# An S4D convolution and a token mixer on one core: the second chunk's selecting table made on chip, weight blocks and x's rows loaded at other places, the first piece's sums on VectorE

## The chip, the cores and the metric

The kernel runs on one core of a Trainium2 chip. The core has TensorE (PE, the matrix engine, whose weight loads are listed apart as PEld), VectorE (DVE), ScalarE (ACT), GpSimd (POOL) and SyncE (SP, which issues most transfers), an on-chip memory of 128 partitions (SBUF), matrix accumulators (PSUM), and 16 DMA engines between them and the memory outside (HBM). The metric is the device time of one execution in microseconds (us), the median over runs. A profiled execution gives the trace; its own time is a little above the median.

## The reference

One block with two halves, on 2048 tokens of 448 channels. The first half is a layer norm with modulation and a long convolution whose kernel comes from 256 complex exponentials per channel, done as an FFT of length 4096. The second is a layer norm and a token-mixing MLP.

```
P = exp((A * dt)[:, :, None] * pos)
K = 2 * einsum("dn,dnl->dl", C, P).real
y = irfft(rfft(u, 2L) * rfft(K, 2L), 2L)[:L]
x = x + ga * (y + u * D_skip)
h = layernorm(x) * (1 + cb) + sb
U = gelu(einsum("sd,sf->df", layernorm(h), w1) + b1)
x = x + gb * (einsum("df,fs->ds", U, w2) + b2)
```

## The kernel before

The FFT of length 4096 is split into 32 frequencies `k1` of 64 points each. The channels go in two chunks of 224. For each chunk there are 16 *pieces*, each of two `k1` values; the second chunk's have the numbers 16 to 31 (`NP` is 16). The first chunk's pieces run beside the generation of the convolution kernel; the second chunk's, which the change is about, run alone in a loop behind it.

A piece passes through these steps. `pc_load(n)` (L749) loads `u`, the input's spectrum, 224 KB, into one of five buffers. `pc_s2(n)` (L780) is eight small matmuls that finish the kernel's spectrum `kx`. `pc_mul(n, e0, e1)` multiplies: VectorE makes the products `zx` and `zy` (L789), and then two engines given as arguments make the difference (L791) and the sum (L792) of the complex product. In before both are GpSimd, for all pieces but the last (31), where both are VectorE. `zx` and `zy` have two buffers each. `pc_tables(n)` (L769, L770) makes the inverse's second table on ScalarE. `pc_inv(n)` (L806) is the inverse transform's eight matmuls, `pc_out(n)` copies the result from PSUM into `vt` on ScalarE (L812) and writes it to the HBM buffer `v_d` (L816), 224 KB. `vt` has four buffers in the second chunk, so the copy of piece n waits for the write of piece n - 4.

The loop takes `m` from 16 to 32 in steps of two (a *round*): matmuls and products of pieces `m` and `m + 1`, then inverse and write of `m - 2` and `m - 1`. PE, ACT, DVE and POOL follow the program's order throughout. SyncE's order is the program's too within this part. All of SP's transfers go through one queue.

Into the loop other loads are woven, in before at these rounds: at 18 the table `fl` (512 KB, L1276); at 20 and 22 `ln_first` (L1179), the first chunk's half of token rows 0 and 1; at 22 and at 24 one block of the MLP's first weights each (`wst.load`, L191; 448 KB in two transfers of 64 partitions); at 28 `x_pair(0)` (L1162), x's rows 0 and 1 (448 KB, also in two transfers).

`fl` is the selecting table. The last transform turns `v_d` into token rows; for rows 0 and 1, the last two pieces' share is taken from their `vt` tiles on chip, not from HBM (`ln_direct`, L1214 and L1216), so that the rows needn't wait for the last writes. `fl` picks out of a `vt` tile's 128 partitions what belongs to row r. It has 128 x 1024 numbers, nearly all zero; others are copies of one small table.

Behind the loop: `ln_second` (L1182) loads the rest of rows 0 and 1, which needs the pieces up to 29 written; `ln_main` (L1222) ends their transform; `ln_load(2)`, `(3)` (L1173) load rows 2 and 3, which need all pieces; then `x_pair(2)`, further weights, the layer norms (`y_sum` L1199, `ln_mod`, `ln_out`) and the MLP (`mlp1`, L1326 to L1328). The norms of rows from 2 on run beside the MLP's first half. A weight block is split by ScalarE (L211) and VectorE (L220) into a high and a low part before use.

Of the kernel before, what the change touches and what calls it, by code (L numbers as in the profile page):

```python
# [22 lines left out]
P = 128  # L23
# [9 lines left out]
NP = 16  # L33
# [6 lines left out]
def dft_tables():  # L40
    n1 = np.arange(32)
    k1 = np.arange(32)
    n2 = np.arange(64)
    k2 = np.arange(64)
    nn = 4096
    t = {}
    w = 2 * np.pi * np.outer(n1, k1) / 64
    w1 = np.zeros((2, 32, 32))
    w1[0] = np.cos(w)
    w1[1] = -np.sin(w)  # L50
    w1[0, :, 0] = 1
    w1[1, :, 0] = (-1.0) ** n1
    wc = np.zeros((4, 32, 2, 4, 32))
    for g in range(4):
        for c in range(2):
            wc[g, :, c, g, :] = w1[c]
    wu = np.zeros((2, 2, 32, 32, 2, 2))
    for a in range(2):
        wu[:, a, ..., a] = w1.transpose(1, 2, 0)
    t["WU"] = wu.reshape(P, P)  # L60

    t["WC"] = wc.reshape(P, 2, 2, 2, 32).swapaxes(3, 4).reshape(P, 2 * P)
    s = np.zeros((2, 64, 32, 2, 64))
    i1 = np.zeros((2, 64, 32, 2, 64))
    i2 = np.zeros((2, 64, 32, 2, 64))

    def inverse(rows, cols, k, m, ang):
        a = np.cos(ang) * 2 / nn
        b = np.sin(ang) * 2 / nn
        i1[0, rows, k, m[0]] = a  # L70
        i1[1, rows, k, m[0]] = -b
        i2[1, rows, k, m[0]] = -a
        i2[0, rows, k, m[0]] = -b
        if len(m) > 1:
            i1[0, rows, k, m[1]] = b
            i1[1, rows, k, m[1]] = a
            i2[1, rows, k, m[1]] = -b
            i2[0, rows, k, m[1]] = a

    for k in range(1, 32):  # L80
        ang = 2 * np.pi * np.outer(n2, k + 64 * k2) / nn
        s[0, :, k, 0] = np.cos(ang)
        s[1, :, k, 0] = np.sin(ang)
        s[0, :, k, 1] = -np.sin(ang)
        s[1, :, k, 1] = np.cos(ang)
        inverse(slice(None), None, k, (0, 1), ang.T)


    for q in range(32):
        ang = 2 * np.pi * n2 * (32 + 64 * q) / nn  # L90
        s[1, :, 0, 0, q] = np.cos(ang)
        s[1, :, 0, 1, q] = -np.sin(ang)
        inverse(q, None, 0, (1,), ang)
    for q in range(33, 64):
        ang = 2 * np.pi * n2 * (64 * (q - 32)) / nn
        s[0, :, 0, 0, q] = np.cos(ang)
        s[0, :, 0, 1, q] = -np.sin(ang)
        inverse(q, None, 0, (0,), ang)
    s[0, :, 0, 0, 32] = 1
    s[0, :, 0, 1, 32] = (-1.0) ** n2  # L100
    i1[0, 32, 0, 0] = 1 / nn
    i2[1, 32, 0, 0] = (-1.0) ** n2 / nn
    s2 = s.reshape(P, 32 * P)

    su = s.swapaxes(3, 4).reshape(2, 64, 32, P)
    t["S2"] = su.reshape(2, 2, 2, 16, 32 * P).swapaxes(1, 2).reshape(P, 32 * P)

    one = np.einsum("cnk,cqkm->km", w1, su)
    t["SV"] = one[ones_k1()].T

    order = lambda a: a.reshape(P, 32, 2, 2, 2, 16).swapaxes(3, 4).reshape(2, 64, 32, P)
    v1, v2 = order(i1), order(i2)
    pairs = v1.reshape(2, 64, NP, 2, P).transpose(3, 1, 2, 0, 4).reshape(P, NP, 2 * P)
    t["SI"] = np.concatenate([s2.reshape(P, NP, 2 * P), pairs], 2).reshape(P, NP * 4 * P)
    t0 = np.zeros((P, 2, P))
    t0[32, 0] = v1[0, 32, 0] + v2[1, 32, 0]
    t0[:, 1] = pairs[:, 0, P:]
    t["T0"] = t0.reshape(P, 2 * P)
    ft = np.zeros((32, 2, 2, 32, 2))
    w = 2 * np.pi * np.outer(k1, n1) / 64  # L120
    f0 = np.cos(w)
    f1 = -np.sin(w)
    f0[0] = 1
    f1[0] = (-1.0) ** n1
    for h in range(2):
        ft[:, 0, h, :, h] = f0
        ft[:, 1, h, :, h] = f1
    t["FT"] = ft.reshape(P, 64)

    fl = np.zeros((2, 2, 2, 16, 2, 4, 2, 32, 2))  # L130
    for r in range(2):
        for g in range(2):
            fl[:, :, g, r, r, :, g] = ft[28:].transpose(1, 2, 0, 3, 4)
    t["FL"] = fl.reshape(P, 8 * P)


    te = np.zeros((3, 64, 16, 32))
    tg = np.zeros((3, 16, 4, 16, 32))
    n = np.arange(32)
    for d in range(16):  # L140
        te[0, 2 * d : 2 * d + 2, d] = 2 * n + 1
        te[2, 2 * d : 2 * d + 2, d] = -n
        tg[0, d, 0:2, d] = n
        tg[0, d, 2:4, d] = 1
        tg[2, d, 0:2, d] = -64 * n
        tg[2, d, 2:4, d] = 1
    tg = tg.reshape(3, 16, 2, 2, 512).swapaxes(1, 2)
    tt = np.concatenate([te.reshape(3, 64, 512), tg.reshape(3, 64, 512)], 1)
    tt[1] = -tt[0]
    t["TT"] = tt.reshape(3, P, 512)  # L150
    return {k: np.ascontiguousarray(v.astype(np.float32)) for k, v in t.items()}


def ones_k1():

    return [0] + list(range(1, 32, 2))
# [7 lines left out]
def token_pair(a, r, g):  # L164

    rows = a.rearrange("(n g h r) d -> g n h (r d)", g=2, h=2, r=16)
    return rows[g, :, :, r * D : (r + 2) * D]
# [58 lines left out]
def tile_adaln_s4d_mixer(ctx, tc, i, out):  # L226
    nc = tc.nc
# [13 lines left out]
    ft = cp.tile([P, 64], F32, name="ft")  # L241
# [5 lines left out]
    with ExitStack() as es:  # L247
        V, S, G, T = nc.vector, nc.scalar, nc.gpsimd, nc.tensor
# [85 lines left out]
        for q in range(4):  # L334
            r = slice(32 * q, 32 * q + 1)
# [422 lines left out]
        def pc_keep(p):  # L758

            nc.sync.dma_start(kept(p)[:, 0 : 3 * P], si[:, p, 0 : 3 * P])  # L760

        def pc_tables(n):

            real, h = pt[n][0], P // 2
            if n == NP:
                pt[n] = real, t0[:, 1]
                return
            imag = fp.tile([P, P], F32, tag="bt", name="bt", bufs=3)
            S.activation(imag[:, 0:h], real[:, h:P], AF.Copy, scale=-1.0)  # L769
            S.copy(imag[:, h:P], real[:, 0:h])  # L770
            pt[n] = real, imag
# [12 lines left out]
        def pc_mul(n, e0, e1):  # L784
            u = pl.pop(n)[0]
            x, y = (fp.tile([P, 2, DC], F32, tag=t, name=t) for t in ("zx", "zy"))
            z = (fp if n < NP else swp).tile([P, 2, DC], F32, tag="z", name="z", bufs=2 if n < NP else 4)
            for j, t in enumerate((x, y)):
                V.tensor_tensor(t, pk[n], u[:, j : j + 1].to_broadcast([P, 2, DC]), ALU.mult)  # L789
            pk.pop(n)  # L790
            e0.tensor_tensor(z[:, 0], x[:, 0], y[:, 1], ALU.subtract)  # L791
            e1.tensor_tensor(z[:, 1], x[:, 1], y[:, 0], ALU.add)  # L792
            pz[n] = z, y
# [358 lines left out]
        wst = WeightStream(tc, ctx, i)  # L1152
# [7 lines left out]
        def x_pair(r):  # L1160
            for g in range(2):
                nc.sync.dma_start(  # L1162
                    xts[r // 2][64 * g : 64 * g + 64].rearrange("p r d -> p (r d)"), token_pair(x, r, g)
                )

        swp = es.enter_context(tc.tile_pool(name="swp", bufs=2, reuse_waits="tile"))
        fl = swp.tile([P, 2, 4, P], F32, name="fl", bufs=1)
# [13 lines left out]
        def ln_second(r, n):  # L1181
            nc.sync.dma_start(vts[r][0:n, :, DC : 2 * DC], v_v[r, 0:n, :, DC : 2 * DC])  # L1182
# [51 lines left out]
        def ln_out(r):  # L1234
# [12 lines left out]
            S.copy(h3h[:, r], h)  # L1247
            return lambda: V.tensor_tensor(h3l[:, r], h, h3h[:, r].bitcast(F32), ALU.subtract)

        last = ExitStack()  # L1250
        last.enter_context(tc.manual_schedule(engines={ENG.SP}))
        for n in (NP + 3, NP + 4):
            pc_load(n)
        pc_keep(NP - 1)
        pc_tables(NP)
        for m in range(NP, 2 * NP + 2, 2):

            if m < 2 * NP:
                for n in (m, m + 1):
                    pc_s2(n)  # L1260
                for n in (m, m + 1):
                    pc_mul(n, *([V, V] if n == 2 * NP - 1 else [G, G]))
                    if n + 1 < 2 * NP:
                        pc_tables(n + 1)
                    if n + 5 < 2 * NP:
                        pc_load(n + 5)
            if m > NP:
                for n in (m - 2, m - 1):
                    pc_inv(n)
                for n in (m - 2, m - 1):  # L1270
                    pc_out(n)
                    if m == 2 * NP and n == m - 2:
                        ln_second(0, 112)
                        ln_second(1, 112)
            if m == NP + 2:
                nc.sync.dma_start(fl, i["FL"].rearrange("p (r j m) -> p r j m", r=2, j=4))  # L1276
            elif m in (NP + 4, NP + 6):
                ln_first((m - NP - 4) // 2)
            if m in (NP + 6, 2 * NP - 8):
                wst.load()  # L1280
            elif m == 2 * NP - 4:
                x_pair(0)

        S.activation(eps_t, eps_t, AF.Sqrt)
        V.memset(eps_t, EPS)
# [22 lines left out]
    with ExitStack() as es:  # L1308
        es.enter_context(tc.manual_schedule(engines={ENG.PE, ENG.Activation, ENG.DVE, ENG.Pool}))
        V, S, G = nc.vector, nc.scalar, nc.gpsimd  # L1310
# [73 lines left out]
        for t in range(16):  # L1384
# [4 lines left out]
            for kh in range(2):  # L1389
                n = 32 + 2 * t + kh  # L1390
# [38 lines left out]
```

## Time and profile before

| | |
|---|---|
| median of 3 runs | 704.68 us (703.97 to 706.22) |
| the profiled execution's own time | 708.53 us |
| its span, first to last instruction | 706.3 us |
| PE busy | 620.9 us, 88% |
| VectorE busy | 453.7 us, 64% |
| ScalarE busy | 438.6 us, 62% |
| GpSimd busy | 271.5 us, 38% |
| moved by DMA | 121.69 MB, mean 172 GB/s |

Busy shares are means over stages that differ: up to about 371 us PE, VectorE, ScalarE and GpSimd share the generation of the convolution kernel, from 371 to 405 the second chunk's pieces run, then come the first rows' norms, and from about 421 to the end the MLP. In the timelines a row gives the start, the duration, the engine, the line, the operation, what it writes and reads, and in brackets how long the engine had been idle and what ended that. A row for SPq is an issue of a transfer; the time is that of the issue, not of the transfer. Rows that follow each other without a gap are merged, with their count.

### The profile page before, as it was taken

What the parts mean: (1) busy time and instruction counts of PE and PEld (TensorE: products, weight loads), DVE (VectorE), ACT (ScalarE), POOL (GpSimd) and SP (SyncE); (2) the same over time, 40 slices, a digit from 0 to 9 for tenths busy, and PEclk for the clock granted to TensorE, in tenths of its full rate; (3) what the DMA queues carried; (4) which work ended last, traced back from release to release, by engine and by line L of the source; (5) the groups of instructions that cost most, each with busy time, mean ns of one, the idle gap of its engine ahead of it and who ended that gap; (6) DMA issues with size and microseconds to landing.
All of it is one profiled execution on the core that took longest, in us unless ns stands there. A gap on an engine that the chain in (4) does not pass through costs nothing. (4 is left out here: it accounts for less than half of the span.)

```text
span 706.3 us, 18230 instructions
## 1 busy us (share of the span) xinstructions
PE 620.9 (88%) x7164; PEld 461.2 (65%) x7164; DVE 453.7 (64%) x877; ACT 438.6 (62%) x876; POOL 271.5 (38%) x326
## 2 busy tenths in 40 slices
PE   0659878889988779798989779999999999999997
PEld 0335445545534556565566647778999999999996
DVE  7469799889679468595866368777622263344441
ACT  5937698888877699998964458888422242222220
POOL 6486548449358768988776300000000000000000
PEclk9968999999998789999899989999999999999999
DMA  7695464468795425444247989984674445555540
GB/s 172 205 192 136 159 216 163 163 219 257 228 301 174 153 73 140 142 131 140 82 118 220 277 226 250 245 202 125 188 226 141 143 128 159 157 156 157 170 131 27
DMA packets 104051, 121.69 MB, mean 172 GB/s; under 512 B 12730, under 2 KB 91758, under 8 KB 103838
## 3 DMA queue, kind: packets, MB, share of 16 engines
q1 hardware_dynamic: 102430, 113.66, 56.1%
q0 software_dynamic: 1536, 6.87, 4.4%
q8 instruction: 57, 0.93, 0.6%
q14 instruction: 28, 0.23, 0.1%
HBM read 85.14 MB, written 34.87 MB: 170 GB/s over the span
## 5 line engine op out<-in xcount | busy, mean ns | idle before, releaser
L211 ACT CAST whi<-w 128x896 fp32r<-128x896 f32 x64 | 59.8, 939 | 135.5 <-PE o L1396 84.7
L655 POOL TENSOR_TENSOR G<-mag,gs 128x512 f32<-128x512 f32 x56 | 72.0, 1286 | 77.7 <-ACT gs L651 77.6
L220 DVE TENSOR_TENSOR wlo<-w,whi 128x896 fp32r<-128x896 f32 x64 | 68.1, 1087 | 40.3 <-ACT whi L211 31.0
L603 PE MATMUL xg<-tab,lph 64*128 64x512 f32 x112 | 66.3, 594 | 21.1 <-issue 7.9
L1326 PE MATMUL acc<-h3h,whi 128*128 128x448 f32 x224 | 83.7, 374 | 0.7 <-ACT h3h L1241 0.7
L1327 PE MATMUL acc<-h3l,whi 128*128 128x448 f32 x224 | 82.3, 368 | 0.0
L686 PEld LDWEIGHTS kg<-E,G 128*32 128x32 f32 x3584 | 59.0, 118 | 35.6 <-issue 16.3
L1328 PE MATMUL acc<-h3h,wlo 128*128 128x448 f32 x224 | 81.5, 364 | 0.0
L1396 PE MATMUL o<-ul,whi 128*128 128x448 f32 x224 | 81.3, 363 | 0.0
L1395 PE MATMUL o<-uh,whi 128*128 128x448 f32 x224 | 81.2, 362 | 0.0
L1397 PE MATMUL o<-uh,wlo 128*128 128x448 f32 x224 | 80.7, 360 | 0.0
L686 PE MATMUL kg<-E,G 128*32 128x64 f32 x3584 | 69.4, 233 | 6.1 <-issue 4.9
L603 PE MATMUL xe<-tab,lph 64*128 64x512 f32 x112 | 65.5, 588 | 10.1 <-ACT gs L652 7.5
L656 POOL TENSOR_TENSOR G<-mag,gs 128x512 f32<-128x512 f32 x56 | 71.9, 1283 | 0.0
L1399 DVE SCALAR_TENSOR_TENSOR y<-o,b,mod 128x448 f32<-128x448 f32 x16 | 10.9, 684 | 80.3 <-PE o L1397 80.3
L632 POOL TENSOR_TENSOR m<-mag,w 128x512 f32<-128x512 f32 x56 | 59.7, 1067 | 6.0 <-DVE E L663 1.5
L657 DVE TENSOR_TENSOR E<-m,xe 128x512 f32<-128x512 f32 x56 | 38.1, 680 | 30.0 <-ACT xe L650 24.0
L640 ACT ACTIVATE ab<-xe 128x512 f32<-128x512 f32 x56 | 34.0, 606 | 31.7 <-PE xe L603 16.6
L1326 PEld LDWEIGHTS acc<-h3h,whi 128*128 128x128 f32 x224 | 42.6, 190 | 14.3 <-issue 3.3
L603 PE MATMUL xe<-tab,lex 64*128 64x512 f32 x56 | 32.8, 598 | 19.4 <-DMA lex<-wm 17.3
L614 ACT ACTIVATE mag<-xe 128x512 f32<-128x512 f32 x56 | 35.5, 633 | 17.0 <-PE xe L603 6.6
L1328 PEld LDWEIGHTS acc<-h3h,wlo 128*128 128x128 f32 x224 | 42.5, 190 | 3.0
(235 smaller groups left out, 1471.6 us busy)
## 6 DMA issues: line engine op xcount, KB each, us to landing
w<-in_B_w_dram SPq DMA_DIRECT2D x64, 224.0 KB
w<-in_B_w_dram SPq DMA_DIRECT2D x32, 448.0 KB
yu_d<-yt SPq DMA_DIRECT2D x16, 448.0 KB
yi<-yu_d SPq DMA_DIRECT2D x16, 448.0 KB
us_d<-uo SPq DMA_DIRECT2D x16, 448.0 KB
u<-us_d SPq DMA_DIRECT2D x32, 224.0 KB
v_d<-vt SPq DMA_DIRECT2D x32, 224.0 KB
vt<-v_d SPq DMA_DIRECT2D x14, 448.0 KB
```

The costliest lines, as they stand in the source:

```text
L211: self.nc.scalar.copy(hi, w)
L220: eng.tensor_tensor(lo, w, hi.bitcast(F32), ALU.subtract)
L603: T.matmul(out[k], lhs[r], rhs[r], start=start, stop=stop)
L655: G.tensor_tensor(Gt[:, 1], mg_, v32(sg), ALU.mult)
L656: G.tensor_tensor(Gt[:, 0], mg_, v32(cg_), ALU.mult)
L686: T.matmul(kgs[g][32 * q : 32 * q + 32, m], Gt[:, c, d], E[:, c, d], start=h == 0 and c == 0 and m == 0, stop=h == 1 and c == 1, skip_grou ...
L1326: nc.tensor.matmul(acc[f], hi[:, fs], h3h[:, r], start=r == 0, stop=False)
L1327: nc.tensor.matmul(acc[f], hi[:, fs], h3l[:, r], start=False, stop=False)
L1328: nc.tensor.matmul(acc[f], lo[:, fs], h3h[:, r], start=False, stop=r == 15)
L1395: nc.tensor.matmul(o, hi[:, ks], uh[kh][:, k], start=kh == 0 and k == 0, stop=False)
L1396: nc.tensor.matmul(o, hi[:, ks], ul[kh][:, k], start=False, stop=False)
L1397: nc.tensor.matmul(o, lo[:, ks], uh[kh][:, k], start=False, stop=kh == 1 and k == 6)
```

## The change

The table `fl` is no longer loaded whole. Its file in HBM shrinks to the small table of 4 x 256 numbers; VectorE clears `fl` on chip ahead of piece 16's products, and four transfers of 4 KB each put the small table at its four places, each into four partitions that lie 32 apart. They are issued by SyncE behind the loads of pieces 19 and 20 and `pc_keep(15)`. Weight block 0 is issued at round 16, behind the loads of pieces 21 and 22, and no longer at 22; block 1 at round 28 and no longer at 24. `x_pair(0)` is issued at round 18, where the table was, and no longer at 28. Piece 16's difference and sum are made by VectorE, as piece 31's are.

```diff
-    fl = np.zeros((2, 2, 2, 16, 2, 4, 2, 32, 2))
-    for r in range(2):
-        for g in range(2):
-            fl[:, :, g, r, r, :, g] = ft[28:].transpose(1, 2, 0, 3, 4)
-    t["FL"] = fl.reshape(P, 8 * P)
+    t["FL"] = ft[28:].transpose(1, 2, 0, 3, 4).reshape(4, 4 * 64)
...
+        def fl_rows():
+
+            V.memset(fl, 0.0)
+            for r in range(2):
+                for g in range(2):
+                    p = 16 * g + r
+                    to = fl[p : p + 97 : 32, r, :, 64 * g : 64 * g + 64]
+                    nc.sync.dma_start(to, i["FL"].rearrange("p (j m) -> p j m", m=64))
...
         pc_tables(NP)
+        fl_rows()
         for m in range(NP, 2 * NP + 2, 2):
...
-                    pc_mul(n, *([V, V] if n == 2 * NP - 1 else [G, G]))
+                    pc_mul(n, *([V, V] if n in (NP, 2 * NP - 1) else [G, G]))
...
-            if m == NP + 2:
-                nc.sync.dma_start(fl, i["FL"].rearrange("p (r j m) -> p r j m", r=2, j=4))
+            if m in (NP, 2 * NP - 4):
+                wst.load()
+            elif m == NP + 2:
+                x_pair(0)
             elif m in (NP + 4, NP + 6):
                 ln_first((m - NP - 4) // 2)
-            if m in (NP + 6, 2 * NP - 8):
-                wst.load()
-            elif m == 2 * NP - 4:
-                x_pair(0)
```

## The prediction

> **What bounds the kernel now.** I read the page first, then a table by stage, then the timelines of the engines between 371 and 425 us, then SyncE's queue. The table by stage (columns: stage and its length, busy time and instruction count of PE, weight load, DVE, ACT and POOL, granted TensorE clock, DMA share, GB/s):
>
> ```profile
> 371.00:380.00 9.00, 8.85 (x82) 5.88 (x76) 6.18 (x11) 2.69 (x15) 5.61 (x9) 1.00 0.49 135
> 380.00:394.00 14.00, 14.00 (x134) 10.32 (x134) 8.66 (x16) 7.57 (x34) 10.90 (x18) 1.00 1.02 296
> 394.00:405.00 11.00, 7.18 (x52) 5.46 (x47) 4.06 (x8) 4.04 (x16) 2.51 (x4) 0.84 1.01 301
> 405.00:415.20 10.20, 6.00 (x35) 3.78 (x33) 5.94 (x17) 6.12 (x12) 0.00 (x0) 0.97 0.64 191
> 415.20:421.00 5.80, 5.80 (x14) 4.06 (x16) 2.95 (x10) 2.69 (x8) 0.00 (x0) 0.50 1.05 248
> 421.00:488.00 67.00, 67.00 (x317) 51.12 (x314) 53.73 (x160) 55.44 (x122) 0.00 (x0) 1.00 0.89 211
> ```
>
> From 421 us on PE has no gap (67.00 of 67.00), so whatever brings that point forward shortens the kernel by as much. The second chunk's pieces 16 to 31 run from 371 to 405. Up to 394 PE is full. From 394 to 405 it works 7.18 of 11 us, while the DMA engines, half idle until 380 (0.49), are full from 380 to 405. TensorE's timeline shows the stalls:
>
> ```profile
> 390.24 1.73 PE L780 MATMUL kx<-yk,yk 128*64 128x224 f32 x16
> ...
> 393.62 1.73 PE L780 MATMUL kx<-yk,yk 128*64 128x224 f32 x16
> 396.95 0.80 PE L806 MATMUL vv<-z,yk 64*128 64x224 f32 x4 [1.60 <-ACT vt L812]
> ...
> 401.10 1.27 PE L806 MATMUL vv<-z,yk 64*128 64x224 f32 x4 [2.21 <-ACT vt L812]
> ...
> 404.49 0.60 PE L1214 MATMUL y<-vt,ft 128*64 128x224 f32 x4
> ...
> 408.40 0.60 PE L1222 MATMUL y<-vt,ft 112*64 112x224 f32 x4 [1.59 <-DMA vt<-v_d]
> ```
>
> One round (two pieces in, the two before them out) takes 393.62 - 390.24 = 3.38 us when nothing waits. The inverses of 28/29 and 30/31 (396.95, 401.10) wait for ACT's copies. What those and VectorE wait for:
>
> ```profile
> 395.32 0.62 DVE L789 TENSOR_TENSOR zx<-kx,u 128x448 f32<-128x448 f32 x1 [2.84 <-DMA u<-us_d]
> ...
> 399.98 0.62 DVE L789 TENSOR_TENSOR zx<-kx,u 128x448 f32<-128x448 f32 x1 [2.45 <-DMA u<-us_d]
> ...
> 418.00 0.62 DVE L1199 SCALAR_TENSOR_TENSOR xt<-xt,y 128x448 f32<-128x448 f32 x1 [2.14 <-DMA xt<-in_A_u_dram]
> ```
>
> ```profile
> 396.46 1.31 ACT L812 COPY vt<-vv 128x224 f32<-128x224 f32 x4 [2.28 <-DMA v_d<-vt]
> ...
> 400.61 1.24 ACT L812 COPY vt<-vv 128x224 f32<-128x224 f32 x4 [2.00 <-DMA v_d<-vt]
> ```
>
> All are transfers: `u` of pieces 29 and 31 on their way in, earlier `vt` on their way out. SyncE's queue shows what they stand behind:
>
> ```profile
> 387.52 1.26 SPq L191 DMA_DIRECT2D w<-in_B_w_dram  x2
> 388.88 1.00 SPq L749 DMA_DIRECT2D u<-us_d  x2
> ...
> 391.53 1.67 SPq L191 DMA_DIRECT2D w<-in_B_w_dram  x2
> 394.07 0.34 SPq L749 DMA_DIRECT2D u<-us_d  x1
> ...
> 405.30 1.28 SPq L1182 DMA_DIRECT2D vt<-v_d  x2
> 406.63 0.59 SPq L816 DMA_DIRECT2D v_d<-vt  x1
> 409.57 1.68 SPq L1173 DMA_DIRECT2D vt<-v_d  x2
> 411.29 1.25 SPq L1162 DMA_DIRECT2D xt<-in_A_u_dram  x2
> ```
>
> `u` of 29 is issued at 388.88, right behind weight block 0, and is there at 395.32: 6.4 us. `u` of 31 follows block 1: 394.07 to 399.98, 5.9 us. The chain behind the pieces is also visible: `ln_second` (405.30) waits until piece 29 is written, `v_d` of 31 (406.63) is queued behind it, `ln_load(2)` and `(3)` (409.57) wait for that write, `x_pair(2)` (411.29) comes behind them, VectorE waits for its rows until 418.00, and 3 us later PE has no gap any more. So **the landing of piece 29's write sets the end**, and the full DMA engines delay it.
>
> **The change part by part.**
>
> *The bytes.* The old table is 524 kB in one load, the new one 16 kB in four. Block 0 (448 KiB, 459 kB) goes from round 22 to round 16, the half idle stretch ahead of 380. `x_pair(0)` and block 1 (459 kB each) change places: the pair takes the table's slot at round 18, block 1 the pair's at round 28. So 508 + 459 = 967 kB leave the full stretch: at its mean of 301 GB/s that is 3.2 us. By stretches, a mix of `u` and `v_d` goes much faster than weights do:
>
> ```profile
> 388.00:390.00 2.00, 2.00 (x24) 1.58 (x19) 1.61 (x3) 1.07 (x5) 1.72 (x4) 1.00 1.06 363
> ...
> 392.00:394.00 2.00, 2.00 (x20) 1.68 (x22) 0.47 (x1) 0.73 (x5) 1.36 (x3) 1.00 1.04 203
> ```
>
> The second row lies where block 0 should be under way, some 4 us after its issue. At 203 GB/s table and block cost 2.5 + 2.3 = 4.8 us. A DMA-bound sum thus gives 3.2 to 4.8 us.
>
> *The pieces once the transfers are in time.* A round's own traffic is four times 229 kB; at 363 GB/s 2.5 us, below PE's 3.38. The table's slot keeps one slow load (the pair), `ln_first` adds 229 kB at rounds 20 and 22, and the rounds' slack of 0.9 us works that off before `u` of 29 and 31. So PE would go on at its own pace: the inverse of 28/29 at 393.62 + 1.73 = 395.35, of 30/31 at 397.0, and L1214 at 398.65 instead of 404.49. At most 5.8 us can be had.
>
> *First piece's sums on VectorE.* Rows of VectorE and then GpSimd at the start of the chunk, and the two sums that VectorE already does for the last piece:
>
> ```profile
> 373.29 0.61 DVE L789 TENSOR_TENSOR zy<-kx,u 128x448 f32<-128x448 f32 x1
> ...
> 375.46 0.62 DVE L789 TENSOR_TENSOR zy<-kx,u 128x448 f32<-128x448 f32 x1 [0.61 <-POOL z L792]
> ...
> 401.17 0.39 DVE L791 TENSOR_TENSOR z<-zx,zy 128x224 f32<-128x224 f32 x1
> 401.48 0.38 DVE L792 TENSOR_TENSOR z<-zx,zy 128x224 f32<-128x224 f32 x1
> ```
>
> ```profile
> 374.16 0.66 POOL L791 TENSOR_TENSOR z<-zx,zy 128x224 f32<-128x224 f32 x1
> 374.77 0.65 POOL L792 TENSOR_TENSOR z<-zx,zy 128x224 f32<-128x224 f32 x1
> ```
>
> Two sums at a spacing of 0.31 us push piece 17's products by 0.62: its `zy` ends at 374.52 instead of 373.90. GpSimd, now free, starts piece 17 at about 374.6 instead of 374.16 (it was still with piece 16), so it ends 0.45 us later. `zy` of 18 waits for exactly that (375.46, released by L792 of piece 17), and PE's inverse of 17 too. For the first inverse I count no gain: two rounds' products, 2 x 1.73 us, keep PE until then. So this edit alone **costs about 0.45 us**; between 0 (if PE finds slack) and 0.8 (two full durations).
>
> *The table made on chip.* No 128 x 1024 f32 clear is in the trace. The nearest row:
>
> ```profile
> L310 DVE MEMSET ones<- 128x512 bf16 x1 | 0.5, 485 | 0.1
> ```
>
> Twice the elements: 0.97 us; four times the bytes: 1.94; I take the first, the row's own rate by elements. It lies in VectorE's idle time:
>
> ```profile
> 371.68 0.62 DVE L789 TENSOR_TENSOR zx<-kx,u 128x448 f32<-128x448 f32 x1 [3.95 <-issue]
> ```
>
> Piece 16's first product has no work ahead of it for 3.95 us, as PE gives its input only then. Nothing is added if the clear starts before 370.7. The four small loads wait on SyncE behind the clear; behind them stand `u` of 21 and all later loads and writes. The queue's rows at this place:
>
> ```profile
> 372.87 5.59 SPq L749 DMA_DIRECT2D u<-us_d  x4
> ...
> 379.54 0.50 SPq L1276 DMA_DIRECT2D fl<-in_FL_dram  x1
> ```
>
> `u` of 21 goes at 372.87 for a product two rounds on, 6.8 us later: four issues at the 0.5 us of the row of the old load, 2 us at most, are covered. Nobody reads the table before 405. Block 0's two issues (1.3 us) fit between `u` of 22 and 23, which waits for VectorE.
>
> *Block 1 at round 28.* It stands straight ahead of the writes of 28 and 29, where the pair stood. With PE's pace shifted by 0.45, the copies of 29 end at about 398.2 and its write is issued at 398.3. In before the same step was
>
> ```profile
> 401.88 0.36 SPq L816 DMA_DIRECT2D v_d<-vt  x1
> ```
>
> and `ln_second` could go at 405.30: 3.4 us. With 3.4 again it goes at 401.7. Shorter, as for the write of 31 (406.63 to 409.57, 2.9), 401.2; as long as the `u` above (6.4), 404.7. I take 3.4, since block 1 in front resembles the pair in front. The gain here is 405.30 - 401.7 = **3.6 us**; ends 0.6 and 4.1, and 5.8 if the chain too shortens.
>
> By the Trainium skill, "DMA: Bandwidth & Descriptors", section "Anatomy of one DMA", a transfer costs about 2.0 us and its bytes at 436 GB/s; the estimate is 2.5 us for this write alone, 3.6 with block 1's bytes ahead of it. The row says 3.4, and no other term would move.
>
> *Behind it* the chain from 405.30 to 421 keeps its steps and its loads, on DMA engines that are at 0.64 in the row of 405 to 415; PE follows. So 3.6 us goes through to the end. The profiled execution takes 708.53 us (span 706.3 and 2.2 around it), 3.85 above the median of 704.68. The sum gives 704.9 for it and 704.68 - 3.6 = **701.1** for the median.
>
> **The rivals.**
>
> *The transfers stay full.* Table and block 0 gone, but pair and two `ln_first` at rounds 18 to 22 keep the queue 6 us deep. For it: 1.02 and 1.01 in both stretches. Against: 967 kB less. The write of 29 then lands 0.6 to 2.0 us sooner: 703.3.
>
> *The clock falls elsewhere.* The clock was at 0.50 in the 415 to 421 row, behind a stretch with 6.00 busy of 10.20. If PE finishes 5.4 us sooner and the write lands only 3.6 sooner, its wait ahead of L1222 grows from 1.59 to about 3.4 us, and the matmuls behind run at half speed: four inverse matmuls took 1.27 cold (401.10) where 0.80 was the most before. That is some 0.5 us on row 0's chain: 701.7. By the Trainium skill, "TensorE: Matmul & The Clock Gate", Part 1, an idle window of about 3.4 us halves the clock, and where the window falls varies from run to run; by that rule this happens in some runs.
>
> *Slower: the clear holds VectorE.* The table's bytes may have belonged to a tile of the first chunk's kernel generation that is released late. VectorE keeps its order, so piece 16's products, GpSimd, PE and every write stand behind the clear. Each us beyond 370.7 for its start costs one. It decides once it passes the 3.6 gained, at 374.3, and is slower by over 0.3% from 376.4. For it: the old load went only at 379.54, so no row shows the bytes free earlier. Against: the generation's last copies on ACT end at 370.08,
>
> ```profile
> 369.01 1.07 ACT L730 COPY yk<-y 128x512 f32<-128x512 f32 x2 [1.03 <-PE y L724]
> ```
>
> and they follow its last matmuls. Held until 377: 707.4.
>
> *It doesn't do what it says:* the traffic taken out was not what held the pieces, and only the first piece's 0.45 remains: 705.1.
>
> **How the numbers follow.** 0.3% of 704.68 is 2.1 us, about what a measurement of this kernel can tell from no change. Forecast (gain 2.1 to 5.8) 0.57, 701.1; clock 0.12, 701.7; transfers stay full 0.17, 703.3; nothing left 0.06, 705.1; slower 0.08, 707.4. Faster by over 0.3% is the first two with a little of the third: 0.70; within 0.22; slower 0.08. The range goes from the most that PE allows, 704.68 - 5.8 = 698.9, rounded to 699.0, to the weak end of the full transfers, a gain of 0.5: 704.2.
>
> **What would show it.** Right: no wait for `u` or `v_d` between 394 and 400, L1214 near 399, `ln_second` issued near 401.7, PE continuous from about 417.5, DMA below full from 384 to 394 and fuller from 374 to 378. First piece: `zy` of 18 near 375.9. Wrong: a wait for `u` of 29 or 31 of over 1 us, a DVE gap around a long clear, or `ln_second` still 6 us behind the write of 29.

## The result, and the profile after

The kernel after takes 699.12 us (median of 20 runs, 694.83 to 706.17), the kernel before 704.08 (20 runs beside it, 697.60 to 711.29). The ratio is 0.9937, with a 95% interval from 0.9912 to 0.9962: 4.4 us faster, between 2.7 and 6.2. It leaves out the executions of either kernel that were over 1.5% above its fastest, so it is not the quotient of the medians, which are 5.0 us apart. Predicted were 3.6 us and a median of 701.1, in a range from 699.0 to 704.2.

The two profiled spans, 706.3 and 695.9 us, differ by 10.4, which is more than the medians do. 5.9 of it lie ahead of the second chunk's first matmul (`kx<-yk,yk`), which starts at 370.60 before and at 364.68 after. In the 14 profiles of this case that start lies anywhere from 361.8 to 370.7, though the work up to it is the same but for the table's clear and its four small loads; in the four profiles without these it lies from 364.9 to 370.6. So from here on times of a profile count **from the chunk's first matmul to the last instruction**: 335.70 before, 331.22 after.

The table by stage of the kernel after, with the columns that were described for before:

```profile
364.68:374.00 9.32, 9.19 (x83) 6.35 (x82) 6.95 (x14) 3.08 (x16) 4.38 (x7) 1.00 0.64 174
374.00:388.00 14.00, 14.00 (x134) 10.32 (x134) 9.66 (x17) 7.52 (x34) 10.82 (x18) 1.00 1.06 339
388.00:394.00 6.00, 5.87 (x52) 4.42 (x49) 3.12 (x6) 4.30 (x17) 2.56 (x4) 1.00 0.85 248
394.00:405.77 11.77, 7.13 (x33) 4.29 (x31) 6.06 (x17) 5.62 (x11) 0.00 (x0) 0.86 0.65 195
405.77:411.60 5.83, 5.65 (x25) 3.98 (x25) 3.14 (x12) 3.17 (x9) 0.00 (x0) 1.00 1.04 262
```

The stretch of 11 us in which PE worked 7.18 us is gone: PE is full until 388 and has 5.87 of the 6 us behind it. The first rows' norms (394 to 405.77) stay a stage in which PE waits. TensorE's timeline of after shows the end of the pieces:

```profile
384.20 1.73 PE L776 MATMUL kx<-yk,yk 128*64 128x224 f32 x16
...
387.58 1.73 PE L776 MATMUL kx<-yk,yk 128*64 128x224 f32 x16
389.25 0.65 PE L802 MATMUL vv<-z,yk 64*128 64x224 f32 x4
...
391.16 0.80 PE L802 MATMUL vv<-z,yk 64*128 64x224 f32 x4
...
393.02 0.60 PE L1210 MATMUL y<-vt,ft 128*64 128x224 f32 x4
393.55 1.78 PE L1212 MATMUL y<-vt,fl 128*128 128x224 f32 x8
398.55 1.01 PE L1218 MATMUL y<-vt,ft 112*64 112x224 f32 x4 [3.22 <-DMA vt<-v_d]
```

The inverses of pieces 28 and 30 start without a wait for a copy, and the selecting table's matmuls come 28.3 us behind the chunk's first (393.02 - 364.68) and not 33.9. But then PE waits 3.22 us for `ln_second`'s rows, where before it waited 1.59: part of what the pieces gained is given back here, as the sum had it. SyncE's queue of after:

```profile
388.77 1.00 SPq L812 DMA_DIRECT2D v_d<-vt  x2
389.82 1.23 SPq L187 DMA_DIRECT2D w<-in_B_w_dram  x2
391.29 1.92 SPq L812 DMA_DIRECT2D v_d<-vt  x3
395.43 1.57 SPq L1178 DMA_DIRECT2D vt<-v_d  x2
397.07 0.58 SPq L812 DMA_DIRECT2D v_d<-vt  x1
400.61 1.22 SPq L1169 DMA_DIRECT2D vt<-v_d  x2
```

From 393.2, the end of the three issues at 391.29, to 395.43 SyncE waits for the write of piece 29, then issues `ln_second`, then the write of 31, and waits again until 400.61 for that. `ln_second` goes 30.75 us behind the chunk's first matmul, before 34.70: 3.95 us sooner, where the sum had 3.6.

### The profile page after: what moved, and what is told of

Read it like the earlier page. It is cut to its first block, busy times and chain, and to the rows that moved or that the text cites. A ratio compares the mean times of both kernels' runs of the same rounds, so it can differ in the third digit from the quotient of the medians.

```text
span 695.9 us, 18229 instructions
## 1 busy us (share of the span) xinstructions
PE 616.3 (89%) x7164; PEld 456.5 (66%) x7164; DVE 459.2 (66%) x880; ACT 438.7 (63%) x876; POOL 270.6 (39%) x324
## 5 line engine op out<-in xcount | busy, mean ns | idle before, releaser
L682 PE MATMUL kg<-E,G 128*32 128x64 f32 x3584 | 68.0, 231 | 3.4 <-issue 2.8
L636 ACT ACTIVATE ab<-xe 128x512 f32<-128x512 f32 x56 | 33.9, 605 | 30.0 <-PE xe L599 18.8
L599 PE MATMUL xe<-tab,lex 64*128 64x512 f32 x56 | 31.4, 570 | 18.9 <-DMA lex<-wm 17.0
L1331 PEld LDWEIGHTS acc<-h3l,whi 128*128 128x128 f32 x224 | 42.1, 188 | 3.8 <-DVE h3l L1244 1.2
```

The source lines that it names most:

```text
L599: T.matmul(out[k], lhs[r], rhs[r], start=start, stop=stop)
L682: T.matmul(kgs[g][32 * q : 32 * q + 32, m], Gt[:, c, d], E[:, c, d], start=h == 0 and c == 0 and m == 0, stop=h == 1 and c == 1, skip_grou ...
L1331: nc.tensor.matmul(acc[f], hi[:, fs], h3l[:, r], start=False, stop=False)
```

## The experiments

Each kernel was profiled and, but for the repeats of before and after, timed against the kernel before. Times in us; the second column is the one that can tell parts apart, since the ratios' intervals are some 0.3 to 0.4% to either side, 2 to 3 us.

| kernel | first matmul of the chunk to the end | to L1214 (table's matmuls) | to `ln_second` | PE's losses up to the MLP | behind it | ratio to before, 95% |
|---|---|---|---|---|---|---|
| before, two profiles | 335.70, 334.40 | 33.89, 32.72 | 34.70, 34.10 | 8.2 + 1.7, 7.4 + 1.7 | 0.0 + 3.1, 0.4 + 1.6 | |
| after, two profiles | 331.22, 331.38 | 28.34, 28.35 | 30.75, 30.41 | 4.9 + 1.7, 4.4 + 1.7 | 1.6 + 0.0, 2.3 + 0.0 | 0.9937 (0.9912 to 0.9962) |
| sums_on_pool | 331.70 | 28.45 | 30.80 | 4.8 + 1.7 | 2.0 + 0.0 | 0.9947 (0.9916 to 0.9979) |
| table_only | 334.60 | 30.96 | 32.69 | 6.4 + 1.7 | 2.2 + 1.7 | 1.0000 (0.9963 to 1.0036) |
| block0_only | 333.33 | 29.46 | 31.66 | 5.1 + 3.1 | 1.9 + 0.0 | 0.9952 (0.9916 to 0.9989) |
| swap_only | 336.85 | 33.81 | 35.49 | 8.3 + 2.6 | 2.0 + 0.7 | 1.0028 (0.9993 to 1.0063) |
| bytes_only | 331.94 | 28.44 | 30.68 | 4.6 + 1.7 | 2.8 + 0.0 | 0.9959 (0.9923 to 0.9996) |
| no_swap | 331.83 | 28.35 | 30.52 | 4.5 + 1.7 | 2.6 + 0.0 | 0.9902 (0.9858 to 0.9946) |
| both_first | 331.08 | 29.95 | 30.99 | 5.8 + 0.0 | 0.1 + 1.7 | 0.9921 (0.9889 to 0.9952) |
| write_first, two profiles | 329.65, 330.42 | 28.34, 28.52 | 30.50, 30.83 | 4.4 + 1.7, 5.0 + 1.6 | 0.7 + 0.0, 0.7 + 0.0 | 0.9943 (0.9906 to 0.9981), 0.9923 (0.9883 to 0.9963) |
| write_pair_first | 331.73 | 28.35 | 30.89 | 5.0 + 3.2 | 0.7 + 0.0 | 0.9939 (0.9897 to 0.9981) |

PE's losses are its idle time, and behind the plus sign the time by which a granted clock below 1.00 stretched its work (busy time times one minus the clock), both summed over windows of half a us of the profile, up to the MLP's first matmul and from there to 64 us behind the chunk's first matmul. Further on, up to the last few us, PE has no gap and the clock is at 1.00. Take the four losses from the time to the end, and 322.7 to 323.5 us are left in every one of the 14 profiles: they account for the differences between the kernels to within some 0.4 us.

### How far the measure repeats

Both kernels unchanged, one more profile each.

> The kernel before, unchanged, for one more profile: how far does the time from the chunk's first matmul to the last instruction (335.70 in the first profile) repeat? If the chunk's part is set by its own order of work, it is within 0.5 us: 335.2 to 336.2. If the free phase of the clock or the memory moves it by as much as the parts of the change, it is off by 1 us or more, and differences of single parts of that size are not to be read.

> The kernel after, unchanged, for one more profile: 331.22 us in the first. Within 0.5 us (330.7 to 331.7) the change's gain of 4.5 us in this part stands as read; a difference of 1 us or more would say that the exchange (0.6) and the sums (0.5) can't be told from nothing by their ends alone.

Before gave 335.70 and 334.40, so it repeats to 1.3 us; its waits for `u` of 29 and 31 were 2.84 and 2.45 us in the one and 2.60 and 2.08 in the other. After gave 331.22 and 331.38. The change's gain in this part is the difference of the means, 335.05 - 331.30 = 3.75 us; by the pairs it lies between 3.0 and 4.5. Before's two profiles differ above all by a stretch of half clock at the start of the MLP, which cost 3.1 us in the one and 1.6 in the other. A single part's effect of 1.5 us or less against before is therefore not to be read from the end alone; landmarks that precede the waits (the rounds' starts) repeat to 0.02.

### The first piece's sums

```diff
-                    pc_mul(n, *([V, V] if n in (NP, 2 * NP - 1) else [G, G]))
+                    pc_mul(n, *([V, V] if n == 2 * NP - 1 else [G, G]))
```

> The kernel after, with piece 16's difference and sum back on GpSimd. Measure: from the chunk's first matmul of L776 to the last instruction (before 706.3 - 370.60 = 335.7 us, after 695.9 - 364.68 = 331.2), since what lies ahead of the chunk differs from run to run. The prediction's step (VectorE's two sums hold piece 17's products up by 0.45 us) expects 330.8, with round 18's products (pieces 20 and 21) 5.46 us behind the first matmul as in before, and all later ones 0.45 sooner than after. The rival, read from the trace of after (round 18 started 0.55 later, but the stall of 0.66 in the next round was gone), expects 331.2 to 331.4: pieces 20 and 21 sooner, pieces 22 and 23 at 9.5 us again as in before.

Round 20's matmuls (pieces 20 and 21; the expectation counts that round as 18) start 5.46 us behind the first with the sums on GpSimd and 6.01 with them on VectorE: the delay that was predicted as 0.45 is there, 0.55. The next round's start at 9.50 and 9.39: the delay is not only made up, it turns into a gain of 0.1, which lasts to L1214 (28.45 and 28.34). Every other kernel with the sums on VectorE shows 6.0 and 9.4, every one with them on GpSimd 5.46 and 9.49 or 9.50. The step that expected 330.8 falls; the end, 331.70, is near the rival's 331.2 to 331.4. VectorE's rows for pieces 18 and 19, first with the sums on GpSimd, then in after:

```profile
369.36 0.62 DVE L785 TENSOR_TENSOR zy<-kx,u 128x448 f32<-128x448 f32 x1 [0.60 <-POOL z L788]
369.90 0.61 DVE L785 TENSOR_TENSOR zx<-kx,u 128x448 f32<-128x448 f32 x1
371.38 0.62 DVE L785 TENSOR_TENSOR zy<-kx,u 128x448 f32<-128x448 f32 x1 [0.87 <-POOL z L788]
```

```profile
370.09 0.62 DVE L785 TENSOR_TENSOR zy<-kx,u 128x448 f32<-128x448 f32 x1 [0.85 <-POOL z L788]
370.63 0.61 DVE L785 TENSOR_TENSOR zx<-kx,u 128x448 f32<-128x448 f32 x1
371.16 0.61 DVE L785 TENSOR_TENSOR zy<-kx,u 128x448 f32<-128x448 f32 x1
```

With the sums on GpSimd there are two waits for it, ahead of `zy` of 18 and of 19; in after the second is gone. GpSimd's own rows say why. `zy` has two buffers. With the sums on GpSimd `zy` of 18 starts as the sum of piece 17 ends (369.32), and `zy` of 19 as the sum of piece 18 ends (371.35): the pieces 17, 18 and 19 share one buffer, and each waits until GpSimd has read the one before. The other buffer is piece 16's, whose `zy` is read once more by its inverse (`pc_inv` has a third term for a chunk's first piece). In after `zy` of 18 waits for piece 17's sum too (it ends at 370.06), but `zy` of 19 starts at 371.16, ahead of piece 18's sum (371.42). So it can't have the same buffer; it has piece 16's, whose inverse is over by then. The edit's cost and its gain are then both a matter of buffers, and its worth is 0.1 us.

### The parts alone

Table on chip only (the table's load at round 18 goes, all else as before):

```diff
         pc_tables(NP)
+        fl_rows()
...
-            if m == NP + 2:
-                nc.sync.dma_start(fl, i["FL"].rearrange("p (r j m) -> p r j m", r=2, j=4))
-            elif m in (NP + 4, NP + 6):
+            if m in (NP + 4, NP + 6):
```

> The kernel before with only the table made on chip: 508 kB fewer at round 18, all else at its old place. If bytes in the full stretch set the end, whichever they are, 508 of the 967 kB give about half of the 4.5 us gained: 333 to 334 us from the chunk's first matmul to the end (before 335.7, after 331.2). If what counts is that weight blocks stand straight ahead of the u of pieces 29 and 31, VectorE's waits of 2.84 and 2.45 us for them stay and it is 335.2 to 335.7.

334.60: between the two expectations, and within the repeats of before. The table's bytes go, but VectorE still waits for `u` of pieces 29 and 31 (its timeline):

```profile
386.51 0.62 DVE L785 TENSOR_TENSOR zx<-kx,u 128x448 f32<-128x448 f32 x1 [0.75 <-DMA u<-us_d]
391.58 0.62 DVE L785 TENSOR_TENSOR zx<-kx,u 128x448 f32<-128x448 f32 x1 [2.44 <-DMA u<-us_d]
```

The first wait fell from 2.84 to 0.75 us, the second stayed. L1214 comes 1.8 to 2.9 us sooner than in the two profiles of before, `ln_second` 1.4 to 2.0; the end shows 1.1 or none of it. The MLP starts 1.3 to 2.0 us sooner than in before, but behind its start PE loses 3.9 us again, half of it at a low clock, where before lost 3.1 and 2.0.

Block 0 at round 16 only:

```diff
-            if m in (NP + 6, 2 * NP - 8):
+            if m in (NP, 2 * NP - 8):
```

> The kernel before with only weight block 0 issued at round 16 in place of 22. By bytes: 459 of 967 kB, about 2.1 us less, 333.6 us from the chunk's first matmul to the end. By position: the wait for u of piece 29 (2.84 us) goes, that for piece 31 (2.45) stays behind block 1; 333 to 334 as well. Against both, the table still at round 18 keeps the queue full, and 335.5.

333.33. Neither wait for `u` of 29 nor of 31 is left, though block 1 still stands at round 24 ahead of piece 31's `u`; what is left is a wait for writes (ScalarE's timeline):

```profile
392.87 1.25 ACT L812 COPY vt<-vv 128x224 f32<-128x224 f32 x4 [0.91 <-DMA v_d<-vt]
```

So a weight block straight ahead of `u` does not make a wait by itself; it does so when it adds to another that is already in the queue. The end is 1.4 us later than in bytes_only (below) although PE idles no longer: 7.0 us against 7.4. The difference is the time lost to half clock behind PE's wait of 2.94 us for `ln_second`'s rows, 3.1 us and not 1.7.

The exchange only (the pair to round 18, behind the table; block 1 to 28):

```diff
-            if m in (NP + 6, 2 * NP - 8):
+            if m in (NP + 6, 2 * NP - 4):
                 wst.load()
-            elif m == 2 * NP - 4:
+            if m == NP + 2:
                 x_pair(0)
```

> The kernel before with only the exchange: x's rows 0 and 1 at round 18 behind the table, block 1 at round 28. The bytes ahead of u of piece 31 are the same (459 kB leave, 459 kB come), so by bytes nothing is gained: 335.4 to 335.9 us from the chunk's first matmul to the end. By position (no weights straight ahead of piece 31's u) the wait of 2.45 us goes and it is 333.5 to 334.5; the pair at round 18 would then cost waits at pieces 25 to 27 instead.

336.85: slower than both profiles of before, by 1.2 and 2.5. No weight block stands ahead of piece 31's `u` any more, and VectorE's wait for that one is gone. But the wait for `u` of piece 29, which still stands behind block 0, grew from 2.84 to 3.73 us, and ScalarE waits for writes (ScalarE, then VectorE):

```profile
383.36 0.59 ACT L812 COPY vt<-vv 128x224 f32<-128x224 f32 x2 [1.70 <-DMA v_d<-vt]
...
393.01 1.23 ACT L812 COPY vt<-vv 128x224 f32<-128x224 f32 x4 [3.18 <-DMA v_d<-vt]
```

```profile
391.85 0.62 DVE L789 TENSOR_TENSOR zx<-kx,u 128x448 f32<-128x448 f32 x1 [3.73 <-DMA u<-us_d]
```

Table and pair together, 983 kB at one place, hold up the writes of the round and, through `vt`'s four buffers, the copies: a new wait of 1.70 us some 18.5 us behind the chunk's first matmul, where before had none, and the late ones are larger than before's. By position alone this should have gained. PE idles 10.3 us in all, in before 8.2 and 7.8.

### The parts in company

Table and block 0 together, no exchange, no sums on VectorE:

```diff
-                    pc_mul(n, *([V, V] if n in (NP, 2 * NP - 1) else [G, G]))
+                    pc_mul(n, *([V, V] if n == 2 * NP - 1 else [G, G]))
...
-            if m in (NP, 2 * NP - 4):
+            if m in (NP, 2 * NP - 8):
                 wst.load()
-            elif m == NP + 2:
+            elif m == 2 * NP - 4:
                 x_pair(0)
```

> The kernel before with the table made on chip and block 0 at round 16, and neither the exchange nor the sums on VectorE: only the 967 kB that leave the full stretch. Profiles of before gave 335.70 and 334.40 us from the chunk's first matmul to the end, of after 331.22 and 331.38. If the bytes are the gain, this one has nearly all of it: 331.2 to 332.2, without waits for u or v_d above 1 us. If the exchange is needed (block 1 stands ahead of piece 31's u here), a wait of 1 us or more for u remains and it is 332.5 to 333.5. Alone, table and block 0 took 1.1 and 2.4 off the first profile: adding gives 332.2 against the first, 330.9 to 332.2 against both.

331.94, with no wait for `u` or `v_d` in the pieces: 3.1 of the 3.75 us. Only the 967 kB that leave the full stretch are moved here, and they bring nearly the whole gain, against which the exchange and the sums together have 0.6. That is half of what before differs by between its two profiles, so it can't be called shown. Up to the MLP PE loses no more than in after; behind its start it idles 2.8 us (after 1.6 and 2.3).

The kernel after without the exchange (the same edit without its first two lines):

> The kernel after without its exchange: block 1 back at round 24, x's rows 0 and 1 back at 28; table on chip, block 0 at round 16 and the sums on VectorE stay. Measure: first matmul of the chunk to the last instruction (before 335.70, after 331.22). If the parts add, the exchange that alone cost 1.15 us costs as much here, and this kernel is at about 330.1. If the exchange is what pays once the queue has room, because block 1 then stands behind u of piece 31, this one is at 332.2 to 333, with VectorE waiting 1 us or more for u of piece 31 again.

331.83, between the two expectations. L1214 is where after has it (28.35), and no wait for `u` is left. So the exchange that costs alone costs nothing once the table is gone, since the pair then takes the table's place and doesn't add to it; what it gains, 0.5, is at the limit.

Both blocks at round 16:

```diff
-            if m in (NP, 2 * NP - 4):
+            if m == NP:
                 wst.load()
+                wst.load()
             elif m == NP + 2:
```

> The kernel after with block 1 too at round 16, straight behind block 0. The prediction's step on block 1 says that it delays the writes of pieces 28 and 29 by its 2.3 us and so ln_second, which then goes 1 to 2 us sooner than after's 30.75 us behind the chunk's first matmul: 29 to 29.7, and the end at 329.5 to 330.2. The rival: 917 kB at round 16 and 459 kB at 18 fill the queue where rounds 20 to 24 need u; waits for u of pieces 23 to 27 appear and the end is at 331.5 to 333.

The rival's waits came, though for writes above all and only once for a `u` (0.96 us, piece 27). ScalarE's timeline:

```profile
376.92 1.26 ACT L808 COPY vt<-vv 128x224 f32<-128x224 f32 x4 [0.77 <-DMA v_d<-vt]
381.58 1.21 ACT L808 COPY vt<-vv 128x224 f32<-128x224 f32 x4 [1.76 <-DMA v_d<-vt]
```

The early rounds lose 1.6 us (L1214 at 29.95), but the other theory is right as well: with nothing between the last writes, `ln_second` goes 1.0 us behind L1214 and not 2.1 to 2.4 as in after and its relatives, so that it is at 30.99 and the end at 331.08, between the two expectations. It goes 2.24 us behind the issue of piece 29's write (391.57, then 393.81), with 459 kB ahead of that write 3.1 to 3.8 us in the 13 other profiles. So a load of that size ahead of the last writes costs over a microsecond, the second block at round 16 a little more; the two cancel.

### A step further: the last write ahead of `ln_second`

In after the write of piece 31 stands on SyncE behind `ln_second`, which itself waits for the write of 29.

```diff
                 for n in (m - 2, m - 1):
                     pc_out(n)
-                    if m == 2 * NP and n == m - 2:
-                        ln_second(0, 112)
-                        ln_second(1, 112)
+                if m == 2 * NP:
+                    ln_second(0, 112)
+                    ln_second(1, 112)
```

> The kernel after with the write of piece 31 issued ahead of ln_second's two loads, no other change. In after the write waited on SyncE from 393.6 (its copy's end) to 397.07 behind ln_second, which itself waited for the write of 29 until 395.43. If the chain named by the prediction (write of 31, ln_load(2) and (3), x_pair(2)) sets the end, the write goes 3 us sooner, ln_load(2) 2 to 3 us sooner than 35.93 us behind the chunk's first matmul, and the end is 1.5 to 2.5 us sooner: 328.7 to 329.7. The rival: ln_second's loads come behind 229 kB and the norm of row 0 sets the end (its first matmul of the MLP at 41.09): 331 to 331.5.

> The kernel after with the write of piece 31 ahead of ln_second, once more: 329.65 us in the first profile, 1.57 sooner than after. The chain theory expects 329.2 to 330.2 again, with ln_load(2) about 33 us behind the chunk's first matmul (after 35.93). Chance in the phase of the clock would give 331 or more.

SyncE's queue in the first of the two:

```profile
397.26 2.68 SPq L812 DMA_DIRECT2D v_d<-vt  x4
401.15 1.28 SPq L1178 DMA_DIRECT2D vt<-v_d  x2
403.69 1.23 SPq L1169 DMA_DIRECT2D vt<-v_d  x2
```

All four last writes go in a row, and `ln_load(2)` 2.5 us behind `ln_second`, not 5.2: 33.04 us behind the chunk's first matmul (370.65 here), 33.28 in the repeat, 35.93 and 35.66 in after. The end comes at 329.65 and 330.42, mean 330.0 against 331.3; the repeat lies between the chain's 329.2 to 330.2 and the 331 of chance. So the chain that the prediction read behind the pieces (write of 31, `ln_load`, `x_pair(2)`) was setting the end, but only half of its 2.6 us reaches it. The MLP's first matmul comes no sooner than in after (40.43 and 41.11; 41.09 and 40.56), since row 0's norm is the later one there, and PE waits 1.19 us for it (row below). What is saved lies behind it: PE waits 0.7 us there and not 1.6 and 2.3.

```profile
411.08 0.48 PE L1330 MATMUL acc<-h3h,whi 128*128 128x448 f32 x1 [1.19 <-ACT h3h L1237]
```

This order is 1.3 us better than after by its profiles and better than before by 0.9943 and 0.9923; the whole runs can't tell it from after (0.9937).

With x's rows 2 and 3 also ahead of `ln_second`:

```diff
                 if m == 2 * NP:
+                    x_pair(2)
                     ln_second(0, 112)
...
-        x_pair(2)
```

> As write_first, and x's rows 2 and 3 (x_pair(2)) issued behind the write of 31 and ahead of ln_second, where SyncE waits anyway. VectorE's wait for them (1.40 us at 43.15) should go: 0.5 to 1 us more than write_first, 328 to 329. The rival: their 459 kB delay ln_second by up to 2 us, row 0's norm comes later, and it is at or above write_first.

The rival holds: 331.73. VectorE's wait for those rows is gone, but the pair's 459 kB are ahead of row 0's, and PE waits for those:

```profile
399.19 1.01 PE L1218 MATMUL y<-vt,ft 112*64 112x224 f32 x4 [3.96 <-DMA vt<-v_d]
```

The MLP's first matmul comes at 42.46, in write_first at 40.43 and 41.11. Most of that is not the wait itself but what follows: at half clock PE loses 3.2 us there, in write_first 1.7 and 1.6; the idle time up to the MLP is 5.0 us, there 4.4 and 5.0. What SyncE's idle time is filled with counts as soon as the DMA engines have work behind it.

## Why the prediction was right, and where it was not

**The mechanism and the size.** The full stretch behind 380 delayed `u` and the writes, and 967 kB taken out of it let PE keep its pace: bytes_only gives 3.1 of 3.75 us with those two edits alone. The measured 3.75 us in the profiles and 4.4 by the ratio stand against 3.6 by the chain, 3.2 to 4.8 by the bytes. That the median of 699.12 is inside the stated range says less: it is 0.1 us from the lower end, and both medians scatter by more. The step that set the size, the landing of piece 29's write, came out as priced. Its issue in SyncE's queue:

```profile
391.78 0.41 SPq L812 DMA_DIRECT2D v_d<-vt  x1
```

`ln_second` at 395.43 is 3.65 us behind it, where 3.4 was taken. The repeat of after has 3.30. The Trainium skill's formula ("DMA: Bandwidth & Descriptors", "Anatomy of one DMA"), which that section fits to transfers issued by GpSimd and not by SyncE, gave as estimates 3.6 with block 1's bytes ahead of it and 2.5 without. The traces are near both: 3.65 and 3.30 in after, 2.24 in both_first.

**What was wrong in the mechanism.** "DMA below full from 384 to 394" failed. The stage row 374 to 388 has 1.06 at 339 GB/s: the queue is as full as before, and a `u` takes about as long, though at the same share the engines moved more (before 296 GB/s at 1.02). SyncE's issues of pieces 29 and 31 and VectorE's product of 29 in after:

```profile
380.94 0.55 SPq L745 DMA_DIRECT2D u<-us_d  x1
...
384.17 0.33 SPq L745 DMA_DIRECT2D u<-us_d  x1
```

```profile
386.79 0.62 DVE L785 TENSOR_TENSOR zx<-kx,u 128x448 f32<-128x448 f32 x1 [0.35 <-DMA u<-us_d]
```

5.85 us, where before had 6.4. What changed is when it was issued: 16.3 us behind the chunk's first matmul and not 18.3, and piece 31's 19.5 (384.17) and not 23.5. The rounds' slack did not drain the queue; the loads moved forward in it.

**How the gain reached the end: right in the number, by luck.** "The chain keeps its steps, PE follows" holds up to the MLP's first matmul, which comes 3.4 us sooner (44.60 and 43.94 before, 41.09 and 40.56 after), nearly all of it idle time of PE. From there on the prediction had the same time in both kernels, and so it came out (291.1 and 290.5 us before, 290.1 and 290.8 after), but only because two terms that it didn't have are of like size. Before had hardly a gap there (5.80 of 5.80 us in the row from 415.20), but a clock of 0.50, which cost 3.1 and 1.6 us in its two profiles. After has the full clock and instead 1.6 and 2.3 us of waits, mostly for VectorE's part of the next rows' norms, so "PE continuous from about 417.5" failed. That they cancel is luck. The low clock at this place goes with a wait: behind the MLP's start it shows in the five profiles in which PE had just waited 1.87 to 2.65 us for row 2's `vt` (both of before, table_only, swap_only, both_first), and in none of the nine others, where that wait was 1.36 us at most. That the wait is its cause is read from this, not tested.

**The first piece's sums: wrong.** The step "this edit alone costs about 0.45 us" is right for one round (0.55) and wrong for the sum (a gain of 0.1), because it followed the wait ahead of piece 18 only and took the next one, ahead of piece 19, for granted. The sum charged 0.45 to all later steps, and they came 0.1 sooner; so the write of piece 29 was issued 0.6 us sooner than in the sum (27.10 behind the chunk's first matmul, 27.7 there), its landing took 0.25 longer, and `ln_second` went 3.95 and not 3.6 us sooner. Between the other pairs of profiles that figure is 3.4 to 4.3, so the surplus itself is within what repeats.

**The table: right.** VectorE's timeline of after:

```profile
361.97 0.91 DVE L1248 MEMSET fl<- 128x1024 f32 x1 [0.16 <-DVE ks L701]
365.76 0.62 DVE L785 TENSOR_TENSOR zx<-kx,u 128x448 f32<-128x448 f32 x1 [2.87 <-issue]
```

The clear takes 0.91 us (0.97 by the row taken, by elements) and starts without waiting for another engine; 2.87 us of idle time are left behind it. The slower rival, a clear that is held, did not come about.

**Block 0 and the exchange.** That block 0 fits into the half idle stretch was right (its DMA share rose from 0.49 to 0.64). The exchange was only counted as a trade of places. In company no cost shows; alone, behind the table, it costs 1.2 to 2.5 us.

**The clock rival came, and cost no more than before's own slow stretch.** PE's wait ahead of L1218 grew to 3.22 us, 3.4 were expected, and the granted clock (the last column but two) fell right there, in two rows of the finer table of after:

```profile
398.00:400.00 2.00, 1.45 (x8) 0.76 (x8) 0.39 (x1) 0.00 (x0) 0.00 (x0) 0.63 0.80 214
400.00:402.00 2.00, 2.00 (x7) 1.61 (x6) 1.81 (x6) 1.05 (x3) 0.00 (x0) 0.51 0.09 11
```

The four matmuls of L1218 took 1.01 us and not 0.60, 0.4 of the 0.5 priced. Over all of PE's work it is 1.65 us, since row 1's matmuls behind them were slow too, and 1.71 in after's second profile, where the wait was 2.78. But before lost 1.65 and 1.71 as well, in the last pieces' inverses (the 1.27 at 401.10): the slow stretch only changed its place. The Trainium skill ("TensorE: Matmul & The Clock Gate", Part 1) has an idle window of about 3.4 us halve the clock. The trace agrees in that it fell at a wait; but none of these waits was as long (3.22 and 2.78 us in after, 2.21 and 1.85 in before), and there the measurement decides.

**Not settled:** the worth of the exchange in company and of the sums (0.6 together), for which the end repeats too coarsely; and how long PE must wait for the clock to fall, which no run here varies by itself.

## What to carry to other kernels

When one queue of transfers is full, move bytes out of the full stretch into a half idle one ahead of it, and don't pile two large loads at one place: the same pair of rows cost over a microsecond behind another load and nothing in that load's stead. Read the delay of a load from where it is issued as much as from how long it takes; here a load kept its 6 us and was in time because it was issued 2 to 4 us sooner. Count the time lost to a low clock apart from the waits: here it was as large as the effects that were being compared. And follow a moved operation through the buffers, not only the engines: which buffer the next tiles are given decided the sign of an edit.

## What the runs showed of the hardware that was not expected

Where a wait of VectorE shows when a `u` of 229 kB was there, it took 5.6 to 6.4 us from issue to use in before's two profiles, and 5.0 to 6.2 in those of after and write_first, though 967 kB had left the stretch: in a full queue the time from issue to landing depended little on what was taken out, and what changed was the time of issue. With the queue run nearly empty a write of the same size let SyncE go on after 2.24 us (both_first).

The time lost to the clock came in amounts: 1.6 to 1.7 us, or about twice that (3.1 to 3.3), or next to nothing, in each of the 14 profiles, up to the MLP and behind it (in swap_only one such stretch of 3.3 lies across the MLP's start). One more or less of these is as large as the effect of one part of this change.

And a profile's start of nearly the same work varied by 8.8 us (361.8 to 370.7) over 14 profiles, twice what the change is worth, while the rounds' starts ahead of the first wait for a transfer repeated to 0.02 us.
